# A dense-attention recurrence beside sliding-window attention: weight residency, streaming ring and stage order rearranged

## Chip, cores, metric

One core of one Trainium2 chip. The metric is the device time of the whole program in microseconds (us); lower is better. The engines have short names: PE is TensorE (matmuls), DVE VectorE, ACT ScalarE, POOL GpSimd, SP SyncE, which here only issues loads and stores. SBUF is the core's working memory, PSUM the memory into which the PE writes. The kernel before takes 2867.67 us (median of 4 runs, 2857.29 to 2870.78).

## The reference

Two independent attentions on the same sequence length, 2048 tokens of width 640, in bf16; their outputs are put side by side.

```python
def _A_ref(x, wqkv, wo):                 # 32 heads of 20, window of 8 keys, dilation 2
    q, k, v = split(x @ wqkv)            # idx = pos - 2 * arange(8)
    logits = einsum('bhsd,bhswd->bhsw', q, k[idx]) * scale
    o = einsum('bhsw,bhswd->bhsd', softmax(mask(logits)), v[idx])
    return merge_heads(o) @ wo

def _B_ref(x, mem0, Wq, Wk, Wv, Wo, seg_len):   # 32 heads of 192, 64 segments of 32 tokens
    mem = mem0                           # 8 memory rows
    for s in range(64):
        h = concat([mem, x[segment s]])  # 40 rows
        q, k, v = h @ Wq, h @ Wk, h @ Wv
        o = attention(q, k, v, mask) @ Wo
        mem = o[:8]; outs.append(o[8:])  # the next segment needs this one's first 8 output rows
```

B is a recurrence: 64 steps that can't overlap. Each step needs all of Wq, Wk, Wv and Wo, 64 "units" of 480 KB (491,520 B), 31 MB in all, which does not fit into SBUF beside the rest. The kernel computes ahead, for all segments at once, the projections of the last 8 rows of each segment, and leaves 32 rows to each step.

## The kernel before

Its order is: load most of B's weights, part A (16 blocks of 128 tokens), precompute B's last rows, load the rest of the weights, the loop of 64 iterations, and a tail that projects the last rows of all segments.

Some units stay in SBUF ("resident"), 20 are read from DRAM again in every iteration ("streamed") through a ring of five tiles ("slots"):

```python
N_STR, N_RING = 20, 5
streamed = [order[int((k + 0.5) * NU / N_STR)] for k in range(N_STR)]   # evenly spaced among 64
...
def done(us):                            # called behind the matmuls that used the units
    for u in us:
        if u in pos:
            k = pos[u] + N_RING          # five streamed units ahead, into the same slot
            op("SP", [], [f"ring{k % N_RING}"], load_ring(k), dma=f"ring{k % N_RING}", ...)
```

`op` only records an operation with what it reads and writes; the waits are worked out from that. Each engine runs its operations in the order of recording. A load can go out only when the PE has finished with the unit that lay in the slot.

The middle of an iteration (`scores` includes the softmax; `turn_p` transposes the probabilities on PE, then copies them out of PSUM as PT, on ScalarE, and PTL, on VectorE; HT is the turned input rows of an iteration, which all its projections read):

```python
vproj(1)
scores(1)        # records softmax 1 on DVE and ACT as well
turn_p(0)        # PE transposes, then the copies PT (ACT) and PTL (DVE)
vproj(2)
pv(0)            # needs PT and PTL
vproj(3)
oproj(0, 0, 4)
turn_p(1)
```

Part A, per block:

```python
nc.sync.dma_start(q[:], q_scr[s0:s0 + 128, :])
nc.sync.dma_start(K8[:], srck)           # 8 keys a token: 128 x 8 runs of 1280 B
nc.gpsimd.dma_start(V8[:], srcv)
nc.vector.tensor_tensor(prod[:], K8[:], q[:].unsqueeze(1)..., op=ALU.mult)
... # sums on PE, softmax, product with V on DVE, sums and output projection on PE
```

## Time and profile before

| stage | from, to (us) | what it does |
|---|---|---|
| weights | 0 to 211 | PE idle |
| part A | 211 to 488 | 16 blocks |
| precompute | 488 to 740 | PE 72% busy |
| reload | 740 to 843 | PE idle |
| loop | 843 to 2782 | 64 iterations of 30.1 us |
| tail | 2782 to 2860 | PE |

First the page of the kernel before: the span in 40 slices, of 71.5 us each. A digit is the busy share in tenths; PEclk is the granted PE clock.

```profile
PE   0006886776217777777777777777777777777767
PEclk9999998987658899898998899899999999899988
DMA  4345775444348999999999999999999999999995
GB/s 137 107 144 173 257 250 174 148 150 132 105 151 306 332 340 346 334 361 328 331 348 332 332 353 345 344 349 346 349 348 347 339 338 343 342 329 352 344 327 167
```

The PE is idle for the first three slices and nearly idle in the eleventh and twelfth. From slice 14 on the picture is flat: the loop, with DMA over 90% and about 330 to 360 GB/s.

The same by stage, from the table of stretches of the kernel before (the loop's stretch was asked from 846 us, 3 us after its first matmul). The columns after the length are busy us of each engine with the number of instructions, then the granted clock, the DMA share and GB/s.

```profile
core 0: us, PE busy (x) PEld busy (x) DVE busy (x) ACT busy (x) POOL busy (x), PEclk, DMA share, GB/s
0.00:211.00 211.00, 0.23 (x3) 0.24 (x4) 1.63 (x5) 1.94 (x2) 1.34 (x7) 1.00 0.43 130
211.00:488.00 277.00, 202.12 (x1544) 124.12 (x1545) 155.76 (x163) 69.32 (x139) 28.54 (x44) 0.91 0.65 219
488.00:740.00 252.00, 182.02 (x872) 82.74 (x859) 58.88 (x134) 51.25 (x130) 2.16 (x12) 0.86 0.44 136
740.00:841.00 101.00, 0.00 (x0) 0.00 (x0) 0.00 (x0) 0.00 (x0) 0.00 (x0) 0.50 0.28 94
846.00:2782.00 1936.00, 1451.98 (x39788) 893.47 (x39788) 801.85 (x2048) 490.41 (x1215) 127.22 (x382) 0.91 0.95 341
2782.00:2860.00 78.00, 54.12 (x384) 38.12 (x384) 5.66 (x9) 12.57 (x9) 0.00 (x0) 0.86 0.54 174
```

What the PE waits for in the loop, from the groups of PE instructions of the kernel before, 1000 to 2600 us (53 iterations): count, busy us and mean ns, then the idle time just before them and what ended it.

```profile
L501 PE MATMUL bank<-w,HT 128*32 128x384 bf16 x8745 | 695.5, 358 | 98.2 <-DVE HT L688 50.8 <-DMA ring<-ws 45.3
L501 PE MATMUL bank<-ring,HT 128*32 128x384 bf16 x3975 | 692.7, 353 | 196.1 <-DMA ring<-ws 195.6
L650 PE MATMUL bank<-ring,buf 128*32 128x160 bf16 x3216 | 113.4, 251 | 25.3 <-DMA ring<-ws 19.1 <-ACT buf L632 0.8
L612 PE MATMUL bank<-PT,Vn 32*128 32x40 bf16 x1712 | 30.6, 183 | 60.5 <-DVE PTL L600 60.5
```

Ring loads are the largest wait (45.3 + 195.6 + 19.1 = 260 us, 4.9 us an iteration), then PTL (1.1 us) and HT (1.0 us). The last line is in the table of DMA issues of the kernel before: size of one transfer and median us from issue to landing.

```profile
ring<-ws SPq DMA_DIRECT2D x1285, 480.0 KB, 5.7
```

This line was on the page when the prediction was made, and its meaning was missed, as will be seen: with five slots at most five transfers of 491,520 B are on their way at a time.

### The profile page before, as it was taken

What the parts mean: (1) busy time and instruction counts of PE and PEld (TensorE: products, weight loads), DVE (VectorE), ACT (ScalarE), POOL (GpSimd) and SP (SyncE); (2) the same over time, 40 slices, a digit from 0 to 9 for tenths busy, and PEclk for the clock granted to TensorE, in tenths of its full rate; (3) what the DMA queues carried; (4) which work ended last, traced back from release to release, by engine and by line L of the source; (5) the groups of instructions that cost most, each with busy time, mean ns of one, the idle gap of its engine ahead of it and who ended that gap; (6) DMA issues with size and microseconds to landing.
All of it is one profiled execution on the core that took longest, in us unless ns stands there. A gap on an engine that the chain in (4) does not pass through costs nothing.

```text
span 2859.7 us, 102330 instructions
## 1 busy us (share of the span) xinstructions
PE 1892.2 (66%) x42592; PEld 1139.3 (40%) x42592; DVE 1023.8 (36%) x2357; ACT 626.0 (22%) x1494; POOL 159.9 (6%) x447
## 2 busy tenths in 40 slices
PE   0006886776217777777777777777777777777767
PEld 0003554333104444444444444444444444444445
DVE  0004664221003434444344344344443444434430
ACT  0002222221002222222222222222222222222221
POOL 0001010000000000000000000000000000000000
PEclk9999998987658899898998899899999999899988
DMA  4345775444348999999999999999999999999995
GB/s 137 107 144 173 257 250 174 148 150 132 105 151 306 332 340 346 334 361 328 331 348 332 332 353 345 344 349 346 349 348 347 339 338 343 342 329 352 344 327 167
DMA packets 360922, 806.29 MB, mean 282 GB/s; under 512 B 54592, under 2 KB 187008, under 8 KB 360880
## 3 DMA queue, kind: packets, MB, share of 16 engines
q1 hardware_dynamic: 334164, 765.12, 76.0%
q0 software_dynamic: 5984, 26.67, 2.6%
q10 hardware_dynamic: 20732, 13.93, 1.6%
q8 instruction: 27, 0.44, 0.1%
q14 instruction: 15, 0.12, 0.0%
HBM read 765.54 MB, written 51.94 MB: 286 GB/s over the span
## 4 chain that ended last, share of the span: by engine, by line
PE 36%; DMA 32%; DVE 12%; SPq 4%; issue 3%; ACT 2%; DVEq 0%; POOLq 0%; ACTq 0%
DMA ring<-ws 22%; PE bank L501 14%; PE bank L650 6%; PE bank L560 3%; PE ps L372 3%; PE bank L534 2%; DMA w<-in_B_Wv_dram 2%; PE yp L730 2%; DVE t L571 2%; DVE t L567 2%; DMA K<-a_kv_scr 2%; DVE mx L570 2%; DVE sm L574 2%; ACT t L573 2%; DMA t<-in_B_Wv_dram 2%
## 5 line engine op out<-in xcount | busy, mean ns | idle before, releaser
L501 PE MATMUL bank<-ring,HT 128*32 128x384 bf16 x4800 | 843.8, 356 | 235.2 <-DMA ring<-ws 232.7
L501 PE MATMUL bank<-w,HT 128*32 128x384 bf16 x10560 | 847.3, 361 | 220.4 <-DMA ring<-ws 156.7
L501 PEld LDWEIGHTS bank<-w,HT 128*32 128x32 bf16 x10560 | 362.2, 103 | 405.0 <-DMA ring<-ws 285.3
L501 PEld LDWEIGHTS bank<-ring,HT 128*32 128x32 bf16 x4800 | 345.5, 101 | 371.4 <-DMA ring<-ws 281.2
L516 DVE CAST nat<-bank 128x384 bf16<-128x384 f32 x256 | 142.3, 556 | 353.5 <-PE bank L501 353.4
L650 PE MATMUL bank<-w,buf 128*32 128x160 bf16 x8448 | 251.7, 251 | 3.2 <-issue 3.2
L516 ACT CAST nat<-bank 128x384 bf16<-128x384 f32 x256 | 121.5, 475 | 579.6 <-PE bank L501 579.5
L539 DVE COPY buf<-bank 128x384 bf16<-128x384 bf16 x256 | 91.0, 356 | 309.9 <-PE bank L534 303.6
L650 PEld LDWEIGHTS bank<-w,buf 128*32 128x32 bf16 x8448 | 185.1, 106 | 22.0 <-issue 14.7
L632 DVE CAST buf<-bank 128x240 bf16<-128x240 f32 x256 | 104.4, 408 | 188.3 <-ACT buf L632 188.3
L534 PE MATMUL bank<-ident,nat 128*128 128x128 bf16 x1536 | 141.2, 233 | 25.8 <-DVE nat L516 25.4
L650 PE MATMUL bank<-ring,buf 128*32 128x160 bf16 x3840 | 135.6, 251 | 30.2 <-DMA ring<-ws 23.1
L539 ACT COPY buf<-bank 128x384 bf16<-128x384 bf16 x256 | 122.6, 479 | 139.7 <-PE bank L534 138.8
L58 PE MATMUL pT<-ident,xb 128*128 128x128 bf16 x80 | 8.3, 241 | 213.7 <-DMA xb<-in_A_x_dram 210.8
L632 ACT CAST buf<-bank 128x240 bf16<-128x240 f32 x256 | 91.7, 358 | 251.9 <-PE bank L626 191.1
L534 PEld LDWEIGHTS bank<-ident,nat 128*128 128x128 bf16 x1536 | 93.9, 103 | 116.7 <-DVE nat L516 51.4
L523 POOL COPY buf<-qkl 128x192 bf16<-128x192 bf16 x256 | 83.4, 347 | 982.1 <-PE bank L560 743.7
L573 ACT ACTIVATE t<-t 128x320 f32<-128x320 f32 x128 | 60.1, 470 | 313.4 <-DVE t L571 313.4
L560 PEld LDWEIGHTS bank<-buf,buf 128*64 128x64 bf16 (+1 forms) x4096 | 104.1, 111 | 45.3 <-issue 41.3
L560 PE MATMUL bank<-buf,buf 128*64 128x40 bf16 (+1 forms) x4096 | 121.0, 187 | 0.0
L65 PE MATMUL pq<-wqkv,xT 128*128 128x480 bf16 x320 | 92.0, 418 | 16.8 <-ACT xT L60 10.0
L387 PE MATMUL ps<-t,XL 128*128 128x384 bf16 x320 | 71.5, 373 | 47.6 <-DMA t<-in_B_Wv_dram 46.6
(106 smaller groups left out, 1979.3 us busy)
## 6 DMA issues: line engine op xcount, KB each, us to landing
ring<-ws SPq DMA_DIRECT2D x1285, 480.0 KB, 5.7
K<-a_kv_scr SPq DMA_DIRECT2D x16, 1280.0 KB
V<-a_kv_scr POOLq DMA_DIRECT2D x16, 1280.0 KB, 8.4
qkl<-qk_scr SPq DMA_DIRECT2D x65, 192.0 KB, 6.3
qk_scr<-st SPq DMA_DIRECT2D x4, 3072.0 KB
t<-ws SPq DMA_DIRECT2D x25, 480.0 KB
v_scr<-vs SPq DMA_DIRECT2D x65, 96.0 KB
vl<-v_scr SPq DMA_DIRECT2D x65, 96.0 KB, 5.7
```

The costliest lines, as they stand in the source:

```text
L65: nc.tensor.matmul(pq[:], lhsT=xT[:, c, :], rhs=wqkv[:, c, g * 480:(g + 1) * 480], start=(c == 0), stop=(c == 4))
L372: nc.tensor.matmul(ps[:], lhsT=w[:, dc, 128 * c:128 * c + 128], rhs=XL[:, dc], start=(dc == 0), stop=(dc == 4))
L387: nc.tensor.matmul(ps[:], lhsT=XLf[:, dc, 128 * tb:128 * tb + 128], rhs=w[:, dc, :], start=(dc == 0), stop=(dc == 4))
L501: i = MM(ps[32 * j:32 * j + 32, :], lhsT=HT[:, dc, :], rhs=ws[j][:, dc, :], start=(dc == 0), stop=(dc == 4), tile_position=(0, 32 * j))
L516: op(e, [b], [f"nat{k}"], lambda s: COPY[e](nats[k][:], ps))
L523: op("POOL", ["qkl"], QPARTS[ty][2:], lambda s, ty=ty: nc.gpsimd.tensor_copy(cells[ty][:, :, :, 32:L], qkl[:, ty, 6 * t:6 * t + 6]))
L534: i = nc.tensor.transpose(tp[ty][:, c], nats[ks[ty]][:, 128 * c:128 * c + 128], ident)
L539: op(e, [("b3", "b5")[ty]], [QPARTS[ty][h]], lambda s, ty=ty, e=e: COPY[e](cells[ty][:, 3 * h:3 * h + 3, :, 0:32], tp[ty].rearrange("p c ( ...
L560: i = MM(Sps[64 * e:64 * e + 64, 4 * rr + j, :], lhsT=QT[lo:hi, o:o + 64], rhs=KT[lo:hi, o:o + L], start=(e not in seen), stop=(n == last[e]),
L573: op("ACT", ["t1"], ["t1"], lambda s: nc.scalar.activation(t1[:], t1[:], ACTF.Exp))
L632: op(e, [f"b{4 + j}"], [f"OT{t}.{j}"], lambda s, e=e, j=j: COPY[e](OTs[t][:, j], ots[j]), also=QPARTS[t])
L650: i = MM(Y[32 * g:32 * g + 32], lhsT=OTs[t][:, j, rr, x, 0:32], rhs=w[:, x, 160 * g:160 * g + 160], start=(t == 0 and n == 0 and x == 0), ...
```

## The change

Its intent: stream less and start earlier. In parts:

1. B's projection weights are kept by groups of four units (j = 0 to 3); all j = 3 units and six O units are streamed: 18 in place of 20, through 6 slots in place of 5.
2. x and A's weights are loaded first; B's groups are loaded from GpSimd's queue during part A; the precompute uses the resident groups, so nothing is reloaded.
3. In A, even and odd tokens are kept apart, so that the 8 keys and values of a token are one run of 20 KB and one load; q stays in SBUF; PSUM tiles are doubled.
4. In the loop the copies PT and PTL of `turn_p(0)` come ahead of softmax 1; small transfers move from SyncE's to ScalarE's queue.
5. To make room, many tiles share memory: the projections' outputs with V, softmax scratch with a K buffer or in PSUM, and so on.

```diff
-    N_STR, N_RING = 20, 5
-    streamed = [order[int((k + 0.5) * NU / N_STR)] for k in range(N_STR)]
+    streamed = [u for u in order if u[0] != O and u[2] == 3 or u in ((O, 1, 0), (O, 0, 2), (O, 0, 3), (O, 2, 0), (O, 3, 1), (O, 2, 3))]
+    N_STR, N_RING = 18, 6
+    SLOT = [k % 6 for k in range(18)]
 ... (part A)
-            nc.sync.dma_start(K8[:], srck)
-            nc.gpsimd.dma_start(V8[:], srcv)
+        nc.sync.dma_start(KV[:].rearrange("p w n -> p (w n)"),
+                          bass.AP(tensor=base.tensor, offset=base.offset, ap=[[2 * D, 128], [1, W * 2 * D]]))
 ... (between A's blocks)
+            load_group(nc.gpsimd, tempg if j == 3 else grp[ty, j], ty, j)
 ... (loop)
     scores(1)
     turn_p(0)
+    softmax(1)
     vproj(2)
 ...
-    op("SP", [], ["vl"], lambda s: nc.sync.dma_start(vl[:]..., v_scr[s + 1]), dma="vl")
+    op("ACT", [], ["vl"], lambda s: nc.scalar.dma_start(vl[:]..., v_scr[s + 1]), dma="vl")
```

(Layouts of the scratch tensors, the tail and the shared tiles are left out.)

## The prediction

> **What bounds the kernel now.** The page's 40 slices and the table of stretches show the stages. (1) Until 211 us the PE is idle: part A's first input sits in SyncE's queue behind part B's weights. (2) Part A, 211 to 488 us: 16 blocks at 14 to 15 us; its chain of waits is kv write (5-6 us), K gather (6 us), DVE multiply (2.8 us), then PE. (3) Precompute, 488 to 740 us, then to 838 us nothing but weight reloads with the PE idle. (4) The recurrent loop, 846 to 2780 us: 64 iterations of 30.2 us. (5) A tail of 80 us, 54 of it PE.
>
> The loop is DMA bound: DMA share 0.95, 343 GB/s, flat over all stretches. An iteration moves 20 streamed units of 491,520 B plus 0.475 MB: 10.31 MB. PE is busy 22.7 us of it; of 7.6 us idle, 4.8 wait for ring loads, 1.2 for PTL behind the second softmax on DVE, 1.0 for HT (groups of lines). Without ring waits: about 25.4 us.
>
> **What the change does.**
> - Start: x and A's weights go first. A starts when wqkv is rearranged (3.55 us a chunk, three on DVE): about 22 us, against 245. Saves about 220 us, all on the critical path.
> - Part A: q stays in SBUF; K and V become one load of 20 KB runs; PSUM is double-buffered. But a KV buffer is held until the block's last transposes, and 13.8 MB of B's weights share the DMA. About 13.5 us a block: A ends near 262 us.
> - Precompute: Q/K 112 us as now (480 matmuls of 0.225 us, plus a stall while st is written). V had to wait for unit loads; now weights are there, but some 27 MB of writes and O loads fall into it: about 80 us, against 140.
> - The 98 us reload disappears; loop set-up 12 us. The loop starts near 467 us, against 846.
> - Loop: 18 units instead of 20, 9.31 MB. At 343 GB/s this is 27.1 us; the PTL wait shrinks because turn_p(0)'s copies now precede softmax 1, so the PE chain is about 24.5 us and DMA still bounds. With imperfect overlap 27.4 us: 64 x 27.4 = 1754, about -180 us. The four small loads moved to ScalarE's queue cost little: it is busy 25%.
> - Tail: larger runs, weights loaded once, but behind 6 MB of raw loads: about 76 us.
>
> The Trainium skill (DMA: Bandwidth & Descriptors, Specifications) gives about 358 GB/s as HBM's limit per core; 343 GB/s at 95% share agrees, so I expect no better rate, only fewer bytes.
>
> **Predicted time.** 467 + 1754 + 76 = 2297 us. Range 2210 to 2380. Faster by over 2%: 0.97; within 2%: 0.02; slower: 0.01.
>
> **What would show it.** A's first PE matmuls near 20 to 25 us. No stretch of idle PE before the loop. Loop start between 420 and 510 us. Iterations of 26.5 to 28.5 us, DMA share 0.93 or more, 335 to 350 GB/s; ring waits still PE's largest wait; the PTL wait for pv(0) mostly gone.
>
> **What would make it wrong.** (a) The loop is PE bound below 27 us, or ring loads stall in bursts, the rate falls under 335 GB/s and an iteration stays at 29. (b) Group loads from GpSimd delay A's KV gathers: blocks of 16 us or more. (c) V's four output buffers wait for slow v_scr writes: over 100 us. (d) New aliases (nat on V, softmax scratch on a K buffer and in PSUM) create waits across engines. (e) Granted clock (0.90 now) falls as the PE gets busier.

## The result, and the profile after

| | before | after |
|---|---|---|
| median us | 2877.35 (15 runs) | 2129.74 (10 runs, 2121.4 to 2135.0) |
| ratio | | 0.7408, 95% interval 0.739 to 0.7427 |
| loop starts (first PE matmul, us) | 843 | 521 |
| iteration, us | 30.08 | 23.60 |
| rate in the loop, GB/s | 342.7 | 394.8 |
| bytes an iteration, MB | 10.31 | 9.32 |
| PE busy, idle an iteration, us | 22.54, 7.54 | 20.34, 3.26 |

A ratio is the mean time of one kernel's fast runs over that of the other's of the same rounds, so it is not quite the ratio of the medians. An iteration is the mean distance between the transposes that make the next HT, over all but the first five and the last three or so; rate, bytes and PE time are taken from the trace in the same stretch.

The changed kernel takes 26% less time, faster as forecast, and outside the predicted range (2210 to 2380). The page of the changed kernel, slices of 53.2 us:

```profile
PE   3777678973788888888888888888888888888849
PEclk9899889986999999999999999999999999999979
DMA  5789875367999999999999999999999999999990
GB/s 199 266 296 308 302 179 173 114 184 253 350 389 392 391 394 394 400 385 395 400 392 396 397 401 398 391 397 385 397 385 401 403 396 392 397 390 399 395 358 14
```

The long idle stretches of the PE are gone, and the flat part is now at 385 to 400 GB/s, not at 340. By stage, the table of stretches of the changed kernel (start, A, Q/K, V and set-up, loop, tail):

```profile
0.00:36.00 36.00, 3.40 (x85) 2.33 (x85) 11.96 (x6) 10.26 (x6) 1.00 (x8) 1.00 0.53 186
36.00:298.00 262.00, 190.12 (x1517) 131.89 (x1518) 141.00 (x144) 72.20 (x160) 20.99 (x39) 0.90 0.81 272
298.00:415.00 117.00, 106.37 (x484) 47.69 (x482) 39.27 (x95) 34.70 (x96) 0.00 (x0) 0.96 0.51 141
415.00:521.00 106.00, 61.82 (x322) 33.28 (x324) 19.11 (x39) 15.39 (x33) 2.88 (x14) 0.80 0.70 213
521.00:2040.00 1519.00, 1305.69 (x39808) 820.97 (x39808) 747.04 (x1920) 507.47 (x1344) 129.53 (x382) 1.00 1.02 393
2040.00:2127.00 87.00, 55.53 (x384) 38.62 (x384) 5.62 (x8) 12.62 (x9) 0.00 (x0) 0.81 0.36 138
```

In the loop the granted clock went from 0.91 to 1.00 and the DMA share from 0.95 to 1.02 (packets overlap a little, so it can pass 1). The groups of PE instructions of the changed kernel, 700 to 1900 us (51 iterations), answer to those of before:

```profile
L505 PE MATMUL bank<-g,HT 128*32 128x384 bf16 x9150 | 591.7, 328 | 90.2 <-DVE HT L701 51.6 <-DMA ring<-ws 18.4 <-DMA temp<-ws 17.9
L535 PE MATMUL bank<-ident,Vn 128*128 128x128 bf16 x1218 | 103.3, 221 | 54.3 <-DVE Vn L520 54.3
L623 PE MATMUL bank<-PT,Vn 32*128 32x40 bf16 x1632 | 27.8, 178 | 0.0
```

Four slots lie in the tile `temp`, two are tiles `ring`. Waits for them are now 0.8 us an iteration in place of 4.9, and the wait for PTL (line 623) is gone. The DMA issues of the changed kernel:

```profile
temp<-ws SPq DMA_DIRECT2D x776, 480.0 KB, 5.7
ring<-ws SPq DMA_DIRECT2D x387, 480.0 KB, 6.4
```

Where the 170 us between 2297 and the profiled 2127 lie:

| part | predicted, us | measured, us | difference |
|---|---|---|---|
| to the loop's start | 467 | 521 | +54 |
| loop | 1754 | 1518 | -236 |
| tail | 76 | 88 | +12 |

So the way to the loop was forecast too short, and the loop far too long; the two errors have opposite signs, so the total hides part of the loop's. The question for the experiments is the loop: why 395 GB/s, when the prediction took 343 for the limit?

### The profile page after: what moved, and what is told of

It reads as the page before. It is cut to its first block, busy times and chain, and to the rows that moved or that the text cites. A ratio compares the mean times of both kernels' runs of the same rounds, so it can differ in the third digit from the quotient of the medians.

```text
span 2127.0 us, 102024 instructions
## 1 busy us (share of the span) xinstructions
PE 1722.9 (81%) x42592; PEld 1074.8 (51%) x42592; DVE 964.0 (45%) x2212; ACT 652.6 (31%) x1645; POOL 154.4 (7%) x443
## 4 chain that ended last, share of the span: by engine, by line
PE 34%; DMA 25%; DVE 18%; issue 4%; ACT 3%; SPq 1%; ACTq 1%; DVEq 0%; POOLq 0%
DMA ring<-ws 20%; PE bank L505 9%; PE bank L661 6%; PE bank L565 5%; PE ps L361 5%; DVE mx L581 3%; DVE sm L585 3%; PE bank L535 3%; PE yp L740 3%; DMA v_scr<-Vn 2%; DVE bank L578 2%; DVE bank L582 2%; DVE XL L582 2%; PE bank L605 2%; DVE XL L578 1%
## 5 line engine op out<-in xcount | busy, mean ns | idle before, releaser
L505 PE MATMUL bank<-g,HT 128*32 128x384 bf16 x11520 | 748.4, 329 | 141.1 <-DVE HT L701 62.8
L505 PEld LDWEIGHTS bank<-g,HT 128*32 128x32 bf16 x11520 | 339.0, 96 | 395.9 <-DMA temp<-ws 174.0
L505 PE MATMUL bank<-temp,HT 128*32 128x384 bf16 x2560 | 491.8, 330 | 0.0
L505 PE MATMUL bank<-ring,HT 128*32 128x384 bf16 x1280 | 252.5, 328 | 0.0
L520 DVE CAST Vn<-bank 128x384 bf16<-128x384 f32 x256 | 142.2, 555 | 224.5 <-PE bank L505 224.5
L661 PE MATMUL bank<-w,XL 128*32 128x160 bf16 x7680 | 212.2, 233 | 12.3 <-ACT XL L643 9.9
L505 PEld LDWEIGHTS bank<-temp,HT 128*32 128x32 bf16 x2560 | 212.9, 96 | 0.0
L535 PE MATMUL bank<-ident,Vn 128*128 128x128 bf16 x1536 | 130.3, 221 | 67.7 <-DVE Vn L520 67.7
L661 PEld LDWEIGHTS bank<-w,XL 128*32 128x32 bf16 x7680 | 147.1, 97 | 37.3 <-ACT XL L643 34.7
L505 PEld LDWEIGHTS bank<-ring,HT 128*32 128x32 bf16 x1280 | 103.0, 96 | 0.0
```

The lines of the kernel that those rows point to most:

```text
L505: i = MM(ps[32 * j:32 * j + 32, :], lhsT=HT[:, dc, :], rhs=ws[j][:, dc, :], start=(dc == 0), stop=(dc == 4), tile_position=(0, 32 * j))
L520: op(e, [b], [f"V{k + 1}"], lambda s: COPY[e](nats[k], ps))
L535: i = nc.tensor.transpose(tp[ty][:, c], nats[ks[ty]][:, 128 * c:128 * c + 128], ident)
L661: i = MM(Y[32 * g:32 * g + 32], lhsT=OTs[t][:, j, rr, x, 0:32], rhs=w[:, x, 160 * g:160 * g + 160], start=(t == 0 and n == 0 and x == 0), ...
```

## The experiments

The theories. **Depth**: the rate is what the ring allows, slots times 480 KB over the time in which a slot goes round, and the sixth slot raised it. **Queue**: the small transfers in SyncE's order held back ring loads. **Placement**: something else, such as where the data lie in DRAM. And, once a run asked for it, **PE order**: the changed place of softmax 1.

### e1 to e4: depth, alone and undone

e1, the changed kernel with the traffic of before:

```diff
-    streamed = [... 18 units ...];  N_STR, N_RING = 18, 6;  SLOT = [k % 6 for k in range(18)]
+    streamed = [... and (O, 1, 1), (O, 2, 2)];  N_STR, N_RING = 20, 5;  SLOT = [k % 5 for k in range(20)]
```

(The tail loads the two units as well.)

> The changed kernel with the loop's weight traffic of before: 20 streamed units and 5 ring slots, all else as changed. Theory depth (the sixth slot keeps the DMA engines fed): the loop falls back to about 343 GB/s, 30 us an iteration, 2530 us in all. Theory queue or placement (something other than depth raised the rate): the rate stays near 393 GB/s, an iteration is 10.3 MB / 393 = 26.2 us, 2300 us in all. Half way (28 us) would say that both matter.

Measured: 2516.61 us (4 runs, 2511.54 to 2525.01), iteration 30.13 us at 341.6 GB/s. That is the iteration of the kernel before (30.08 us, 342.7 GB/s), with every other change of the loop in place. The table of stretches, 700 to 1900 us, and one group of PE instructions of e1:

```profile
700.00:1900.00 1200.00, 946.20 (x24778) 572.51 (x24774) 465.05 (x1197) 316.06 (x836) 82.56 (x240) 0.84 0.95 341
```

```profile
L661 PE MATMUL bank<-temp,XL 128*32 128x160 bf16 x2880 | 106.7, 262 | 129.0 <-DMA temp<-ws 128.7
```

The share 0.95 and the rate are those of before, and the PE waits for the ring again. Queue and placement, both still as in the changed kernel, can't carry the gain by themselves. What e1 changed is the number of units and slots, and with it which units are streamed.

That e1 lands on just the old iteration is partly luck. It keeps the new place of softmax 1, and that alone takes the kernel before, with the same 20 units and five slots, to 28.9 us (e10, below). So something else in the changed kernel costs about 1.2 us an iteration when the ring has five slots. Its streamed units are not spread evenly, its small transfers are on ScalarE's queue (in the kernel before that alone went with 30.8 us, e4), and its granted clock was 0.84 against 0.95 in e10; which of these it is was not tried.

e2, five slots for the 18 units:

```diff
-    N_STR, N_RING = 18, 6;  SLOT = [k % 6 for k in range(18)]
+    N_STR, N_RING = 18, 5;  SLOT = [0,1,2,3,4, 0,1,2,3,4, 0,1,2,3,4, 1,2,3]
```

> The changed kernel with 18 units but only 5 ring slots. Theory depth: the rate drops clearly, iteration 26 us or more, 2280 us. Theory queue or placement: iteration stays at 23.6 to 24.2 us, 2130 to 2170 us.

Measured: 2399.95 us (2387.38 to 2409.55), iteration 27.80 us at 335.2 GB/s. So one slot is worth up to 4.2 us an iteration, 270 us in all. "Up to", since the test has a flaw that was seen only afterwards: 18 is no multiple of 5, and a unit's slot is fixed in the loop's code, so at the turn of the iteration loads go out in another order than they are used (unit 0 of the next round ahead of unit 15). 27.8 us is near the 27.4 us that the prediction had for "fewer bytes at the same rate", but with the disturbed order and a rate of 335.2 GB/s this is no evidence that its sum was right.

e3, a sixth slot in the kernel before:

```diff
-    N_STR, N_RING = 20, 5
+    N_STR, N_RING = 20, 6
+    SLOT = [0, 1, 2, 3, 4, 5, 0, 1, 3, 4, 2, 5, 0, 3, 4, 1, 2, 5, 3, 4]
```

> The kernel before with a sixth ring slot, 20 units as they were (5 to 7 units of distance). Theory depth: iteration from 30.2 to about 27 us, 2660 us in all. Theory queue or placement: within 1% of before.

Measured: 2865.24 us, ratio 0.9967 (0.9899 to 1.0035), iteration 30.34 us. A miss for depth as it was put. But it has the flaw of e2: 20 isn't a multiple of 6, so the load for unit 15 goes out when unit 7 is done, ahead of unit 13's, and takes the DMA engines' time first. The run is inconclusive by itself; e5 and e6 do it in order.

e4, the small transfers alone:

```diff
-    op("SP", [], ["qkl"], lambda s: nc.sync.dma_start(...
+    op("ACT", [], ["qkl"], lambda s: nc.scalar.dma_start(...      # and vl, ol, yo likewise
```

> The kernel before with only its four small loop transfers (left scores, left values, left outputs, output rows) issued from ScalarE's queue instead of SyncE's. Theory queue (those in-order waits hold back ring loads, or one queue alone can't fill the engines): rate up towards 390 GB/s, iteration 27 us or less, 2660 us. Theories depth and placement: within 1% of before.

Measured: 2893.72 us, ratio 1.0076 (1.0003 to 1.0149), 334.9 GB/s. The queue doesn't raise the rate.

### e5 to e8: depth in order

In the kernel before 18 units and 6 slots don't fit into SBUF (39.5 KB asked for where 35.1 are left). More units and more slots do, as each streamed unit frees its resident tile. Each of these is one line:

```diff
-    N_STR, N_RING = 20, 5
+    N_STR, N_RING = 24, 6      # e5;  24, 8 in e6;  20, 4 in e7
```

> The sixth slot in the kernel before was not a clean test: 20 units don't divide by 6, so loads were issued out of the order of use. Here 24 units in 6 slots, strictly in order; 12.27 MB an iteration. Theory depth (distance of 6 loads ahead, in order, fills the DMA engines): about 390 GB/s, iteration 31.5 us, 2940 us in all. Theory that something else in the changed kernel is needed for the rate: 343 GB/s, iteration 35.8 us, 3220 us.

> As the last, but 8 slots. Theory depth: saturated like 6 slots or a little better, 390 to 400 GB/s, iteration 31 us. If depth matters but 6 is not the limit in this kernel, this is clearly faster than 6 slots. Rival: 343 GB/s as with 5 slots.

> The kernel before with 4 slots in place of 5, in order. Theory depth: the rate falls by about as much again, to 280 to 300 GB/s, iteration 35 us, 3180 us. Rival (the rate in the kernel before is set by something else, such as HBM or the queue): within 2% of before.

Measured: e5 3032.91 us, e6 2892.74 us, e7 3160.56 us. With the kernel before, as read from the traces:

| units, slots | iteration, us | MB | GB/s | DMA share | issue to landing, us | time a slot goes round, us |
|---|---|---|---|---|---|---|
| 20, 4 (e7) | 35.22 | 10.31 | 292.7 | 0.850 | 4.8 | 7.0 |
| 20, 5 (before) | 30.08 | 10.31 | 342.7 | 0.953 | 5.7 | 7.5 |
| 24, 6 (e5) | 32.90 | 12.26 | 372.6 | 0.977 | 6.0 | 8.2 |
| 24, 8 (e6) | 30.81 | 12.28 | 398.6 | 1.020 | 7.7 | 10.3 |

The last column is slots times iteration over units, 5 x 30.08 / 20 = 7.5. The landing times are these lines of the tables of DMA issues, of e7, e5 and e6:

```profile
ring<-ws SPq DMA_DIRECT2D x1284, 480.0 KB, 4.8
```

```profile
ring<-ws SPq DMA_DIRECT2D x1542, 480.0 KB, 6.0
```

```profile
ring<-ws SPq DMA_DIRECT2D x1544, 480.0 KB, 7.7
```

Two steps change the slots alone: from 4 to 5 at 20 units the rate rises from 292.7 to 342.7 GB/s, and from 6 to 8 at 24 units from 372.6 to 398.6, where the engines are full. The step from 5 to 6 changes the number of units as well, and e3, six slots for 20 units, gained nothing in its disturbed order; so what the sixth slot alone is worth isn't shown in the kernel before. e6 streams 19% more bytes than the kernel before in an iteration of nearly the same length. So 343 GB/s was not a limit of the memory or of the DMA engines; it was what five slots gave with the PE freeing them as it did. A slot is busy while its load is on its way and some 2 us longer: the unit waits for its turn, is read, and the next load is issued. e5 came short of the 390 GB/s that was expected (372.6), so six slots alone don't fill the engines in the kernel before.

e8, the small transfers of the changed kernel back on SyncE's queue:

> The changed kernel with its four small loop transfers back on SyncE's queue. Theory depth: within 1.5% of the changed kernel, 2130 to 2160 us. Theory queue (it helps only when the ring is deep enough): back towards 27 us an iteration, 2350 us.

```diff
-    op("ACT", [], ["qkl"], lambda s: nc.scalar.dma_start(...
+    op("SP", [], ["qkl"], lambda s: nc.sync.dma_start(...         # and vl, ol, z likewise
```

Measured: 2154.88 us, iteration 24.02 us. Its ratio to the kernel before is 0.7493 against 0.7408 for the changed kernel: the queue is worth about 1%.

### e9: fewer bytes, fewer slots

Two units fewer in the stream and two slots fewer take the same SBUF. By bytes alone this is better, by depth worse.

```diff
-    N_STR, N_RING = 18, 6;  SLOT = [k % 6 for k in range(18)]
+    N_STR, N_RING = 16, 4;  SLOT = [k % 4 for k in range(16)]     # (O,0,3) and (O,2,3) resident
```

> The changed kernel with two units fewer in the stream and two slots fewer, which is the same SBUF: 16 units, 8.33 MB an iteration, in order, 4 loads ahead. Theory bytes (the prediction's: the loop costs bytes over a fixed rate): faster than the changed kernel, 8.33 MB / 393 = 21.2 us, held at the PE's 22.8 us, 2080 us in all. Theory depth (the rate is slots over a load's round trip, 293 GB/s at 4 slots as in the kernel before): 28.4 us an iteration, 2440 us.

Measured: 2335.75 us (2318.19 to 2343.7), iteration 26.83 us at 310.2 GB/s: 8.32 MB take longer than 9.32 MB. The sign is depth's. The size isn't: 26.83 us in place of 28.4. Four slots give 310 GB/s here and 293 in e7, so something in the changed kernel makes slots go round faster. That is the next question.

### e10, e13, e14: the place of softmax 1

e10, only that part of the change, in the kernel before:

```diff
     scores(1)        # without its softmax
     turn_p(0)
+    softmax(1)
     vproj(2)
```

> The kernel before with only the order of the loop changed: the copies of turn_p(0) ahead of softmax 1, as in the changed kernel. Theory depth: the PE's wait for PTL (1.2 us an iteration) disappears and comes back as waits for ring loads; within 1% of before, 2850 to 2890 us. Rival (the PE chain is part of what limits the loop): about 1.2 us x 64 = 75 us faster, 2800 us.

Measured: 2794.09 us, ratio 0.9706 (0.9669 to 0.9744), iteration 28.89 us at 356.8 GB/s. The size is the rival's, and the depth theory as it was put missed. From the groups of PE instructions of e10, 1000 to 2600 us (55 iterations):

```profile
L616 PE MATMUL bank<-PT,Vn 32*128 32x40 bf16 x1760 | 30.5, 180 | 0.0
L501 PE MATMUL bank<-w,HT 128*32 128x384 bf16 x9165 | 698.1, 346 | 125.0 <-DMA ring<-ws 65.7 <-DVE HT L694 57.2
L501 PE MATMUL bank<-ring,HT 128*32 128x384 bf16 x4163 | 694.9, 345 | 182.5 <-DMA ring<-ws 182.0
L654 PE MATMUL bank<-ring,buf 128*32 128x160 bf16 x3300 | 111.7, 243 | 53.3 <-DMA ring<-ws 47.8
```

And the tables of stretches, 1000 to 2600 us, of the kernel before and of e10:

```profile
1000.00:2600.00 1600.00, 1198.92 (x33145) 739.24 (x33134) 664.95 (x1698) 407.06 (x1009) 106.22 (x319) 0.92 0.95 342
1000.00:2600.00 1600.00, 1213.62 (x34423) 740.10 (x34423) 691.69 (x1778) 428.38 (x1053) 111.84 (x332) 0.95 0.97 357
```

In the kernel before the first group waited 60.5 us for PTL, 1.1 us an iteration, and now it doesn't wait. About 0.45 us of this came back as waits for ring loads, as the depth theory said (65.7 + 182.0 + 47.8 = 295.5 us, 5.3 us an iteration in place of 4.9). What it did not foresee is the PE's work, which fell from 22.5 to 21.9 us an iteration, at a granted clock of 0.95 in place of 0.92. So of the 1.2 us gained about half is idle time and half is PE time. That the gain is as large as the PTL wait was is a coincidence of these two. A reading that fits, though no run shows it directly: while the PE stands still no slot comes free, so a stall with few slots also delays loads.

Is that so with a full ring too? e13 undoes the order in the changed kernel, six slots kept:

```diff
-    turn_p(0)
-    softmax(1)
+    turn_p(0, lambda: softmax(1))    # transposes on PE, softmax 1, then the copies PT and PTL
```

> The changed kernel with softmax 1 again ahead of turn_p(0)'s two copies, 6 slots kept. If a saturated DMA hides a PE wait: iteration 23.6 to 23.9 us, within 1%, 2130 to 2150 us. If the loop is a chain of PE and slots at any depth: the 1.1 us of e10 comes back, 24.7 us, 2200 us.

Measured: 2347.98 us (2343.8 to 2363.62), iteration 27.06 us: 3.5 us more, three times the larger of the two expectations. The table of stretches of e13, 700 to 1900 us, and the group that tells why:

```profile
700.00:1900.00 1200.00, 955.98 (x27573) 615.58 (x27570) 518.32 (x1330) 354.65 (x933) 86.90 (x265) 0.94 0.92 343
```

```profile
L625 PE MATMUL bank<-PT,Vn 32*128 32x40 bf16 x1440 | 25.6, 182 | 114.5 <-DVE XL L613 114.5
```

The PE waits 114.5 us for PTL (which lies in the tile XL here) in 44 iterations, 2.6 us each, where the kernel before waited 1.1. A reading that fits and was not tested: there, the PE got to this place late, because `vproj(2)` had waited for its ring load; with the loads in time the wait for DVE shows in full. The rest of the 3.5 us is PE time, 21.58 us an iteration in place of 20.34, at a granted clock of 0.94 in place of 1.00. The DMA share is down to 0.92 and ring waits are only 0.72 us: with the old order this kernel is bound by the PE's own chain, 27.06 - 0.72 = 26.3 us, at a rate that happens to be 343 GB/s again.

e14, the order alone where eight slots keep the engines full:

> e6 (kernel before, 24 units, 8 slots, 30.8 us an iteration at 399 GB/s) with e10's order. If a saturated DMA hides PE waits: 30.3 to 30.8 us, 2870 to 2895 us. If not: 29.7 us, 2825 us.

Measured: 2880.71 us, iteration 30.55 us at 401.7 GB/s, against e6's 30.81 us and 398.6. In e6 the wait was long:

```profile
L612 PE MATMUL bank<-PT,Vn 32*128 32x40 bf16 x1648 | 30.9, 190 | 127.6 <-DVE PTL L600 127.6
```

127.6 us in 52 iterations, 2.5 us each. Taking it away brings 0.26 us; waits for loads rise from 3.94 to 5.00 us an iteration, and a new wait for a copy on VectorE takes 1.0 us (50.8 us in 52 iterations). Here the engines are the limit, 12.27 MB at about 400 GB/s, and the iteration hardly moves when the PE's stall goes.

So the same edit is worth 1.2, 3.5 and 0.3 us an iteration, in loops that the traces show bound by a shallow ring, by the PE's chain, and by full DMA engines. The granted clock moved with it, 0.92 to 0.95, 0.94 to 1.00 and 0.88 to 0.92, and no run separates its part.

### e11 and e12: part A

Part A came out at 14.6 us a block, not 13.5. Every second block has a group load beside it. e11 gives these loads to the end of A:

```diff
-        if i >= 3 and i % 2 and early:
+        while i == 17 and early:
```

> The changed kernel with the seven group loads moved from the middle of part A to its end. If these loads delay A's KV loads (the prediction's point b): blocks of A at 12.7 us in place of 14.6, A ends about 28 us earlier, but some 40 us of loads then stand ahead of the Q stage, so 2140 us in all. If they don't: blocks stay at 14.6 us and the whole is 40 us slower, 2170 us.

Measured: 2171.32 us; blocks of 13.9 us (208.8 us from the first to the sixteenth output in place of 219.4). VectorE's wait for its KV load in part A fell from 14.9 to 3.8 us, these two lines of the lists of waits, of the changed kernel (60 to 298 us) and of e11 (60 to 290 us):

```profile
DVE KV L95 <- DMA KV<-a_kv_scr: 14.9, 6, 4.3
```

```profile
DVE KV L95 <- DMA KV<-a_kv_scr: 3.8, 3, 1.8
```

So the loads cost A about 11 us, less than expected, and they are better there than later. Even without them a block takes as long as one of the kernel before (13.9 us from output to output there too): A as rearranged, longer runs included, is no shorter. Its timeline suggests a chain from DVE to PE to ACT and back; that was not tested.

e12 issues them from ScalarE:

```diff
-            load_group(nc.gpsimd, tempg if j == 3 else grp[ty, j], ty, j)
+            load_group(nc.scalar, tempg if j == 3 else grp[ty, j], ty, j)
```

> The changed kernel with the group loads issued from ScalarE's queue in place of GpSimd's, at the same places. If it is GpSimd's descriptor path that costs: A's blocks with a load shorten to about 13 us and the whole is 10 to 15 us faster. If it is the shared DMA engines alone: within 0.5% of the changed kernel.

Measured: 2179.04 us, blocks of 17.2 us: both expectations missed, in the other direction. The list of waits of e12, 60 to 335 us:

```profile
DVE KV L95 <- DMA KV<-a_kv_scr: 89.2, 12, 14.2
ACT lg L101 <- DMA g<-in_B_Wq_dram: 15.3, 1, 15.3
```

The KV loads land late beside group loads on ScalarE's queue, 89 us of waits in place of 15. Why these crowd out the KV loads more than GpSimd's do was not tried, and stays open. Nothing here points to GpSimd's queue as what slowed A.

### e15 to e17: the V stage, and a better version

In the V stage the chain of waits of the changed kernel is mostly writes of V's results (2.2% of the span, some 47 us), from four buffers. e15 uses 12, cut from the two ring tiles, which have nothing in them yet:

```diff
+    ring45 = [cst.tile([128, US], BF16, name=f"ring{k}")[:] for k in (4, 5)]
+    vss += [t[:, 384 * n:384 * n + 384] for t in ring45 for n in range(5)][:8]
-                cps[tb % 2](vss[tb], ps[:])
+                cps[tb % 2](vss[(16 * j + 4 * r + tb) % 12], ps[:])
```

> The changed kernel with 12 in place of 4 output buffers in the V stage, cut from the two ring tiles that are still unused there. If V waits for its v_scr writes (the prediction's point c): the V stage falls from 85 to 60 to 70 us and the whole to 2105 to 2115 us. If the DMA engines or the O loads hold V: within 0.3% of the changed kernel.

Measured: 2132.7 us. The loop did start 20 us earlier (500.5 us in place of 521.0), and then ran at 23.98 us an iteration in place of 23.60, which took all of it back. e15 allocates the ring tiles earlier, so they lie elsewhere. e16 allocates the small tiles ahead of them, so that all keep their addresses; e17 is the changed kernel once more, on the same chip.

> As e15, but the ring tiles and all small tiles keep the addresses that they have in the changed kernel. If e15's slower loop came from the moved tiles: loop 23.6 us, 2105 to 2115 us. If the loop simply varies between builds: 23.6 to 24.0 us, 2110 to 2135 us.

> The changed kernel unchanged: 2121 to 2135 us, loop 23.5 to 23.7 us. If its profile now shows 23.8 us or more, e15's difference is run-to-run variation.

Measured: e16 2119.94 us (2111.51 to 2121.51, 6 runs), iteration 23.69 us, loop from 501.4 us; e17 2131.2 us (2125.22 to 2135.2, 6 runs), iteration 23.68 us, loop from 518.5 us. The runs of the two don't overlap. e16 is the fastest version, 0.5% below the changed kernel. That moved ring tiles slow the loop fits e15 and e16 but isn't shown: the loops of e11 and e12, whose tiles didn't move, took 23.90 and 23.84 us. What sets these last 0.3 us is open.

## Why the prediction was wrong

The direction was right and its largest step, the rate in the loop, was wrong.

- **The step that failed.** The prediction said: "343 GB/s at 95% share agrees, so I expect no better rate, only fewer bytes", hence 9.31 MB in 27.1 us and "with imperfect overlap 27.4 us". The rate was 394.8 GB/s and the iteration 23.60 us: -236 us. What it took for the limit of the memory was set by the ring: five slots going round in 7.5 us give 5 x 491,520 B / 7.5 us = 328 GB/s of ring loads, plus 16 for the small transfers. This sum alone proves nothing, since the 7.5 us come from the iteration itself. The slots show it: at 20 units 4 and 5 slots gave 293 and 343 GB/s, at 24 units 6 and 8 gave 373 and 399; in the changed kernel, 20 units in 5 slots brought back 341.6 GB/s and an iteration of 30.1 us (partly by luck, see e1). The prediction never weighed the sixth slot, nor that the PE's stalls bear on the rate (five slots gave 357 GB/s in e10, without the PTL wait).
- **A figure taken as support.** The Trainium skill (DMA: Bandwidth & Descriptors, Specifications) gives about 358 GB/s as HBM's limit per core, which is a stack's bandwidth divided by two cores. The same page says further down (Bandwidth, Measured) that a core gets roughly this when both cores of the pair are streaming. This program runs on one core, so the figure was not its limit, and the prediction used it without that condition. It happened to lie close to 343, and so the busy share of 0.95 was read as "nearly at the limit". One core reached 395 to 402 GB/s here (the changed kernel, e6, e14).
- **The PE's chain.** Predicted without ring waits: about 24.5 us. Measured: 23.60 - 0.78 = 22.8 us. That the PTL wait goes was right. Its worth wasn't: the prediction let DMA hide it, but undone in the changed kernel it costs 3.5 us (e13). Both are needed: with five slots the loop falls to 27.8 us (e2, with its flaw), with the old order to 27.1 us, with both in place it is 23.6 us. The DMA engines are then full (share 1.02), and the PE is busy for 20.3 of 23.6 us.
- **The clock, point (e).** It was feared that a busier PE is granted less. It was granted more: 0.91 before, 1.00 after in the loop, and PE's work in an iteration shrank from 22.54 to 20.34 us (the same 128x384 matmul took 358 ns before and 328 after, on average). The Trainium skill (TensorE: Matmul & The Clock Gate, Part 1) says that activity releases the throttle and idle time brings it back; the runs agree at the ends: 0.81 in e7, with 9.5 us of idle PE an iteration, 1.00 after, with 3.3 us. In between they don't fall in order: the kernel before had 7.5 us idle at 0.91, e1 only 6.4 us at 0.84. So the amount of idle time alone doesn't tell the granted clock here, and what else sets it is open. In the changed kernel and in e10 less waiting and less PE time came together; how much of the gain is clock alone can't be taken apart, since nothing here sets the clock by itself.
- **The four small loads on ScalarE's queue.** "Cost little" was right: 1% gain in the changed kernel (e8), 0.8% loss in the kernel before (e4).
- **Start and part A.** Predicted: A's first projections at 22 us, blocks of 13.5 us, end at 262 us. Measured: 36.2, 14.6 and 298 us. The rearranging of wqkv on DVE (10.5 us) waited for B's x and began at 20.7 us, and what the PE waited for last was ScalarE's copy of A's turned x, which began at 35.4 us, behind loads of wo; of the block time, about 0.7 us is the group loads (e11, point (b) in a mild form); the rest is that a block got no shorter than before, 13.9 us.
- **Precompute.** Q/K 117 us against 112. V and set-up 106 us against 92: V did wait for its four buffers (point (c)), and 12 buffers brought the loop's start 20 us forward (e15, e16). No reload was right.
- **Tail.** 88 us against 76: the first matmul comes 24 us after the loop, behind the raw loads, in place of 19 us. This was foreseen as a cost and sized too small.
- **Aliases, point (d).** They appear as a wait of PE for DVE's copy into V's memory (54.3 us in 51 iterations, 1.1 us each, 0.4 before in the like place) and not as more. They paid for the sixth slot, which wouldn't fit otherwise.

## What to carry to other kernels

A flat bandwidth with DMA engines 95% busy isn't yet the memory's limit. Bytes in flight (slots x size) over the time in which a slot goes round tell where the time of a load goes, but can't settle it: a ring that is always refilled gives the rate that you see in any case (8 x 491,520 B / 10.3 us = 382 GB/s of ring loads in e6, where the engines were full). What settles it is a run with another number of slots, in steps that divide the number of loads, so that loads stay in the order of use. And expect a stall on one engine to be worth anything from a tenth of its length to more than all of it (here 0.26 us for a wait of 2.5, 1.2 for 1.1, 3.5 for 2.6): its worth depends on whether a shallow ring, that engine's own chain, or a full transfer path bounds the loop at that moment, so price such steps together and not one by one.

## What the Trainium skill lacked or had wrong

- DMA: Bandwidth & Descriptors (Specifications): the row of about 358 GB/s doesn't say that it is for two cores streaming; the page says so only further down (Bandwidth, Measured). Read without that, it misled the prediction: one core moved 394.8 GB/s over the whole loop of the changed kernel, nearly all of it reads, and 398.6 and 401.7 GB/s in e6 and e14.
- No page that I found says how many transfers must be in flight. With 480 KB each, 4 and 5 gave 293 and 343 GB/s (20 loads an iteration), 6 and 8 gave 373 and 399 (24 loads) in the loop of the kernel before, and the time from issue to landing grew from 4.8 to 7.7 us.
- DMA: Bandwidth & Descriptors (Issuing engine by pattern): "HWDGE (sync/scalar) is generally faster" did not hold for the program as a whole. Seven groups of 2.0 MB issued from ScalarE beside other large loads made the kernel 2.3% slower than from GpSimd (2179.04 against 2129.74 us), with 89 us in place of 15 us of waits for those other loads. Why is open.
- TensorE: Matmul & The Clock Gate (Part 1): that idle time brings the throttle back agrees in kind, but more idle time an iteration didn't always mean less clock: 7.5 us and 0.91 in the kernel before, 6.4 us and 0.84 in e1.
